# One core, windowed attention with sink tokens and a highway layer: ScalarE copy ahead of the second exponential, another start order, and crossbar transposes for eight blocks

## The chip, the cores and the metric

The kernel runs on one core of one Trainium2 chip. The metric is the device time of one execution in microseconds (us); less is better. A kernel is run several times, and each run has a span (first to last instruction, some 1.7 us less than the device time) and the mean clock that TensorE was granted, as a share of full speed. A stretch for which a trace holds no clock record counts as full in that mean and in the PEclk columns below. Runs over 1.5% above the fastest of the same kernel are set aside as slow. Engine names: PE is TensorE (matmuls and transposes by matmul), ACT is ScalarE, DVE is VectorE, POOL is GpSimd, SP is SyncE. PEld is PE's weight load, which overlaps PE. A "q" after the name (SPq, POOLq) is the engine's sequencer, which issues transfers.

## The reference

Attention with 4 sink positions and a window of 128, for 4 batches, 8 heads, 768 positions, head size 64; then a highway layer over 3072 tokens of 512 features.

```python
scores = q @ k.T / sqrt(64);  keep = is_sink | in_window
a = exp(scores - max) ; a = a / (sum(a) + 1e-9) ; x = a @ v          # x: 3072 x 512
H = maximum(x @ w_h, 0) ; T = 1 / (1 + exp(-(x @ w_t + b_t)))
out = T * H + (1 - T) * x
```

## The kernel before

The tokens are worked off in 24 blocks of 128, six to a batch. A block needs its own keys and those of the block before; the first of a batch has no block before, so its scores are half as large. Block n goes through these pieces:

| piece | engine | what it does | PSUM pool |
|---|---|---|---|
| T | PE, ACT copy `act_T` | transposes of q and k, copied to SBUF as `qk` | m |
| S, two halves | PE, ACT exponential `act_S`, DVE mask | scores, `e = exp(...)` | s |
| sk | PE, ACT short exponential | scores against the sinks, of two blocks at once | m |
| A | PE, then DVE `rec`, `x` | `e @ v`, division by the sum, giving `xh` | av |
| X | PE, ACT copy `act_X` | transpose of x, giving `xT` | m |
| Mt | PE, ACT tanh `act_u` | gate matmuls (`tps`) | m |
| Mh | PE, DVE `d`, `e`, `o` | candidate matmuls (`hps`), combination, store | m |

The engines take their instructions in the order in which the program lists them (weight loads aside), and the pool m has two buffers of one PSUM bank each that T, X, Mt, Mh and sk take in turn.

```python
s_ps  = ...tile_pool(name="ps_s",  bufs=2, space=PSUM)
av_ps = ...tile_pool(name="ps_av", bufs=1, space=PSUM)
m_ps  = ...tile_pool(name="ps_m",  bufs=2, space=PSUM)
...
for i in range(-2, NB + 2):                # a step; ms, os_: blocks whose Mt/Mh or d/e/o are due
    ...
    if has_sink(i): act_sink(i)
    if on(i + 1):
        pe_S(i + 1, 0); act_S(i + 1, 0); pe_S(i + 1, 1)
    if on(i - 1) and i - 1 not in XBAR:
        pe_X(i - 1); act_X(i - 1)
    for o in os_: dve_d(o)
    if on(i): dve_mask(i, 1)
    if on(i + 1): act_S(i + 1, 1)          # ACT: second exponential ...
    if on(i + 2): pe_T(i + 2)
    for o in os_: dve_e(o)
    if on(i): pe_A(i)
    if on(i + 2): act_T(i + 2)             # ... and only then the q,k copy
    if on(i + 1): dve_mask(i + 1, 0)
    if on(i): dve_rec(i)
    for o in os_: dve_o(o)
    if on(i):
        dve_x(i)
        if i in XBAR: sp_X(i)              # XBAR is empty here
    for m in ms:
        pe_Mt(m); act_u(m); pe_Mh(m)
    if has_sink(i + 1): pe_sink(i + 1)
    ...                                    # loads of block i + 10, POOL queue
```

(The `pe_` calls are shown several to a line; the start-up constants and the issue of the loads are cut.)

The softmax here doesn't subtract the row's maximum and nothing guards it: scores larger than these inputs give would overflow.

## Time and profile before

| what | before |
|---|---|
| time, median | 146.31 us |
| span of the profiled run | 145.0 us |
| six blocks in mid-run | 30.0 us |
| PE / ACT / DVE busy in these 30.0 us | 26.9 / 24.0 / 22.6 us |

The chain of waits of the kernel before, cut to one step in mid-run. Columns: start in us, length in us, what.

```profile
53.12 1.11 ACT e L251
54.23 0.47 ACT xT L315
54.71 1.02 ACT e L251
55.73 0.91 ACT qk L203
56.68 1.02 PE hps L336 x4
```

Four ACT instructions stand in a row, then PE's Mh (`hps`), and after it the next scores (in this step those against the sinks come first) start the next row. The list of waits of the kernel before shows the same tie from both ends. Columns: who waited for whom, us in total, times, longest us.

```profile
DVE dd L342 <- PE hps L336: 26.2, 24, 1.5
ACT e L251 <- PE sps L243: 12.7, 16, 0.9
PE hps L336 <- ACT qk L203: 9.4, 17, 0.7
```

Mh does not use the q,k copy's data. It waits for it because T and Mh take the same buffer of pool m in turn, and the copy is what frees it. While PE waits there, nothing releases ACT's next exponential, so ACT waits later.

Busy time by stretches of the kernel before. The columns are given in the first line.

```profile
core 0: us, PE busy (x) PEld busy (x) DVE busy (x) ACT busy (x) POOL busy (x), PEclk, DMA share, GB/s
43.40:73.40 30.00, 26.85 (x328) 17.65 (x328) 22.56 (x42) 23.96 (x32) 21.08 (x28) 1.00 1.87 170
73.40:103.40 30.00, 26.85 (x327) 17.66 (x326) 22.57 (x42) 23.96 (x32) 12.53 (x17) 1.00 0.98 106
```

The two stretches are six blocks each, with the same busy times. No engine is full (PE, the fullest, is busy for 26.85 of 30.00 us). The start is another matter; this is the timeline of the kernel before around the transposes of block 2.

```profile
11.04 1.04 PE L243 MATMUL sps<-qk 64*128 64x128 f16 x16 [1.10 <-ACT qk L203]
18.77 0.61 PE L196 MATMUL tp<-ident,qsd 128*128 128x128 f16 x4 [6.70 <-DMA qsd<-in_q_dram]
19.60 0.61 PE L198 MATMUL tp<-ident,ksd 128*128 128x128 f16 x4 [0.22 <-DMA ksd<-in_k_dram]
```

PE stands idle for 6.70 us until the q and k of block 2 have landed, although blocks 0 and 1 still have work that needs none of it.

### The profile page before, as it was taken

Reading aid. Unit: us, or ns where it says so; the run is one execution under the profiler, and the core shown is the slowest. Engines: PE = TensorE matmul, PEld = TensorE weight load, DVE = VectorE, ACT = ScalarE, POOL = GpSimd, SP = SyncE. Lnnn points to the kernel's source line nnn. Section 1 sums busy time; section 2 is a strip of 40 time slices with the busy share of each in tenths; the row PEclk is TensorE's granted clock in tenths of the full one; section 3 lists DMA queues with packets and bytes.
Section 4 is the critical chain, followed back from the end, with each engine's and each line's share of the span. In section 5 each row is a group of like instructions: output and inputs, shape, how many; then the busy total and the mean of one; then the engine's idle time right before and its main releaser. Section 6 shows DMA issues by size and latency. Waiting matters only on the chain.

```text
span 145.0 us, 3266 instructions
## 1 busy us (share of the span) xinstructions
PE 115.4 (80%) x1312; PEld 74.8 (52%) x1312; DVE 96.9 (67%) x214; ACT 98.0 (68%) x129; POOL 73.6 (51%) x98
## 2 busy tenths in 40 slices
PE   6632069989889988988899789889897988998840
PEld 2122058557646654765666358458464664664410
DVE  7441016578659856966868687678677866968770
ACT  3176029497787877977976797798769778976310
POOL 6999599999969999735099770000300000000000
PEclk9975555899999999999999999999999999999996
DMA  1999999999999999999929999210221021021111
GB/s 10 113 112 168 165 155 158 153 156 197 163 190 195 191 183 150 195 194 152 74 74 147 150 197 161 73 73 3 75 77 72 1 77 72 0 77 72 72 72 72
DMA packets 79728, 17.00 MB, mean 117 GB/s; under 512 B 75617, under 2 KB 76641, under 8 KB 79714
## 3 DMA queue, kind: packets, MB, share of 16 engines
q0 software_dynamic: 76256, 10.51, 107.8%
q1 hardware_dynamic: 3458, 6.30, 12.1%
q8 instruction: 10, 0.16, 0.4%
q14 instruction: 4, 0.03, 0.1%
HBM read 21.01 MB, written 6.29 MB: 188 GB/s over the span
## 4 chain that ended last, share of the span: by engine, by line
ACT 41%; PE 35%; POOL 7%; DMA 5%; issue 5%; DVE 4%; POOLq 0%; DVEq 0%
ACT e L251 25%; PE hps L336 16%; ACT qk L203 11%; DMA ksd<-in_k_dram 5%; PE tps L323 4%; ACT xT L315 4%; PE av L277 4%; PE sps L243 4%; DVE dd L342 3%; PE sk L221 3%; POOL qsd L85 2%; PE tps L321 1%; POOL ksd L86 1%; POOL v L93 1%; PE tp L198 1%
## 5 line engine op out<-in xcount | busy, mean ns | idle before, releaser
L251 ACT ACTIVATE e<-sps,ebias 128x1024 f16<-128x1024 f32 (+1 forms) x48 | 49.8, 1041 | 12.7 <-PE sps L243 12.7
L342 DVE SCALAR_TENSOR_TENSOR dd<-hps,xh 128x512 f16<-128x512 f32 x24 | 16.6, 692 | 26.2 <-PE hps L336 26.2
L262 DVE TENSOR_TENSOR e<-e,mask 128x1024 f16<-128x1024 f16 (+1 forms) x48 | 30.7, 640 | 4.4 <-ACT e L251 4.0
L203 ACT COPY qk<-tp 128x1024 f16<-128x1024 f16 x24 | 24.3, 1015 | 11.7 <-PE tp L198 11.7
L336 PE MATMUL hps<-wh_sb,xT 128*128 128x512 f16 x96 | 24.6, 378 | 9.4 <-ACT qk L203 9.4
L85 POOL DMA_DIRECT2D qsd<-in_q_dram x24 | 22.4, 932 | 7.6 <-PE tp L198 5.0
L323 PE MATMUL tps<-wt_sb,xT 128*128 128x512 f16 x96 | 25.0, 383 | 0.0
L277 PE MATMUL av<-v,e 128*128 128x112 f16 x352 | 24.4, 218 | 0.7 <-DVE e L262 0.7
L86 POOL DMA_DIRECT2D ksd<-in_k_dram x24 | 22.2, 925 | 1.1 <-PE av L283 1.0
L93 POOL DMA_DIRECT2D v<-in_v_dram x24 | 22.5, 937 | 0.0
L277 PEld LDWEIGHTS <-e 128*128 128x128 f16 x352 | 21.3, 101 | 1.1 <-DVE e L262 0.9
L336 PEld LDWEIGHTS <-xT 128*128 128x128 f16 x96 | 9.3, 97 | 23.5 <-issue 14.1
L329 ACT ACTIVATE u<-tps 128x512 f16<-128x512 f32 x24 | 14.7, 613 | 6.9 <-PE tps L323 6.8
L243 PE MATMUL sps<-qk 64*128 64x128 f16 x352 | 14.8, 225 | 2.6 <-ACT qk L203 2.6
L348 DVE SCALAR_TENSOR_TENSOR ee<-u,dd 128x512 f16<-128x512 f16 x24 | 16.5, 686 | 0.2
L296 DVE TENSOR_TENSOR xh<-av,rec 128x512 f16<-128x512 f32 x24 | 16.4, 685 | 0.1
L196 PE MATMUL tp<-ident,qsd 128*128 128x128 f16 x96 | 9.9, 230 | 7.2 <-DMA qsd<-in_q_dram 6.9
L354 DVE SCALAR_TENSOR_TENSOR otok<-xh,ee 128x512 f32<-128x512 f16 x24 | 15.6, 648 | 0.1
L243 PEld LDWEIGHTS <-qk 64*128 64x128 f16 x352 | 10.7, 98 | 9.4 <-issue 7.3
L323 PEld LDWEIGHTS <-xT 128*128 128x128 f16 x96 | 9.5, 99 | 11.0 <-issue 1.8
L315 ACT COPY xT<-xtp 128x512 f16<-128x512 f16 x24 | 13.7, 572 | 1.0 <-PE xtp L310 1.0
L212 POOL COPY ks<-qk 64x16 f16<-64x16 f16 x8 | 1.6, 201 | 21.1 <-ACT qk L203 20.9
(49 smaller groups left out, 103.3 us busy)
## 6 DMA issues: line engine op xcount, KB each, us to landing
out_dram<-otok SPq DMA_DIRECT2D x24, 256.0 KB, 2.2
qsd<-in_q_dram POOLq DMA_DIRECT2D x24, 128.0 KB, 5.7
ksd<-in_k_dram POOLq DMA_DIRECT2D x24, 128.0 KB, 5.7
v<-in_v_dram POOLq DMA_DIRECT2D x24, 128.0 KB, 6.1
wt_sb<-in_moe_w_t_dram POOLq DMA_DIRECT2D x1, 512.0 KB, 6.7
wh_sb<-in_moe_w_h_dram POOLq DMA_DIRECT2D x1, 512.0 KB, 8.8
vd<-in_v_dram POOLq DMA_DIRECT2D x4, 4.0 KB, 4.2
bt<-in_moe_b_t_dram SPq DMA_DIRECT2D x1, 2.0 KB
```

The lines of the kernel that those rows point to most:

```text
L85: nc.gpsimd.dma_start(out=qsd, in_=q[b, :, rows, :].transpose([1, 0, 2]))
L86: nc.gpsimd.dma_start(out=ksd, in_=k[b, :, rows, :].transpose([1, 0, 2]))
L93: nc.gpsimd.dma_start(out=vt[:, :, 0:D], in_=v[b, :, rows, :].transpose([1, 0, 2]))
L203: nc.scalar.copy(out=qk, in_=tp_of.pop(n))
L243: nc.tensor.matmul(sps[:, hh, o:o + P], lhsT=kk[rows, hp, :], rhs=qT[rows, hp, :], start=True, stop=True)
L251: nc.scalar.activation(out=e.rearrange("p a b c d -> p a (b c d)"), in_=sps[:, :, 0:2 * np_ * P], func=AF.Exp, bias=ebias, scale=SCALE)
L262: nc.vector.tensor_tensor(out=ev, in0=ev, in1=m.unsqueeze(1).to_broadcast([P, 4, np_ * P]), op=ALU.mult)
L277: nc.tensor.matmul(av[:, g, 2 * hl + hh, 0:_AVN], lhsT=e[:, hh, hl, pc, :], rhs=vt[:, 65 * h:65 * h + _AVN], start=first, stop=False, skip ...
L315: nc.scalar.copy(out=xT, in_=xtp_of.pop(n))
L323: nc.tensor.matmul(tps, lhsT=xT[:, kc, :], rhs=wt_sb[:, kc, :], start=False, stop=(kc == NOC - 1))
L336: nc.tensor.matmul(hps, lhsT=xT[:, kc, :], rhs=wh_sb[:, kc, :], start=(kc == 0), stop=(kc == NOC - 1))
L342: nc.vector.scalar_tensor_tensor(out=dd, in0=h_of.pop(n), scalar=0.0, in1=xh_of[n], op0=ALU.max, op1=ALU.subtract)
```

## The change

Three things, as the diff has them: from step 2 on, ACT takes the q,k copy ahead of the second exponential; in the start, blocks 0 and 1 are carried on before the transposes of block 2; and blocks 14 to 21 have x transposed by a DMA through the crossbar (`sp_X`, present but unused before) instead of PE and an ACT copy. Such a block's Mt and Mh come one step later (lag 2).

```diff
--- before.py
+++ after.py
@@ -73,7 +73,7 @@
     NV = AHEAD + 4
     NS4 = H * NSINK
     KW = NHP * P + 32
-    XBAR = ()
+    XBAR = range(14, 22)
     v_ring = [const.tile([P, VW], FP16, tag=f"v{i}", name=f"v{i}") for i in range(NV)]
     qk_sd = {}
 
@@ -375,7 +375,7 @@
                 more_constants()
             if has_sink(i):
                 act_sink(i)
-            if on(i + 1):
+            if i >= 2 and on(i + 1):
                 pe_S(i + 1, 0)
                 act_S(i + 1, 0)
                 pe_S(i + 1, 1)
@@ -383,20 +383,20 @@
                 pe_X(i - 1)
                 act_X(i - 1)
             for o in os_:
-                dve_d(o)
+                if o not in dd_of:
+                    dve_d(o)
             if on(i):
                 dve_mask(i, 1)
-            if on(i + 1):
+            if i >= 2 and on(i + 2):
+                pe_T(i + 2)
+                act_T(i + 2)
+            if i >= 2 and on(i + 1):
                 act_S(i + 1, 1)
-            if on(i + 2):
-                pe_T(i + 2)
             for o in os_:
                 dve_e(o)
             if on(i):
                 pe_A(i)
-            if on(i + 2):
-                act_T(i + 2)
-            if on(i + 1):
+            if i >= 2 and on(i + 1):
                 dve_mask(i + 1, 0)
             if on(i):
                 dve_rec(i)
@@ -410,6 +410,20 @@
                 pe_Mt(m)
                 act_u(m)
                 pe_Mh(m)
+            if i == 1:
+                dve_d(0)
+                pe_T(2)
+                act_T(2)
+            if -1 <= i < 2:
+                for g in range(2):
+                    pe_S(i + 1, g)
+                    act_S(i + 1, g)
+                dve_mask(i + 1, 0)
+            if i < 2:
+                n = {-2: 0, -1: 1, 1: 3}.get(i)
+                if n is not None:
+                    pe_T(n)
+                    act_T(n)
             if has_sink(i + 1):
                 pe_sink(i + 1)
             if i == 0:
@@ -422,7 +436,7 @@
                     sink_v(b, nc.gpsimd)
                 if b + 1 < B:
                     load_sink_v(b + 1)
-            for n in (range(3, AHEAD + 1) if i == -2 else [i + 2 + AHEAD]):
+            for n in {-2: range(3, AHEAD + 1), 0: [], 1: [10, 11]}.get(i, [i + 2 + AHEAD]):
                 if n < NB:
                     if n > 3:
                         load_qk(n)
```

## The prediction

> **What bounds the kernel.** The chain of waits repeats one pattern per block in mid-run: PE scores (0.35 us to the first half), ScalarE first exponential 1.11, xT copy 0.47, second exponential 1.02, q,k copy 0.91, PE Mh (the hps matmuls) 1.02, next scores: 4.95 us, about 5.4 with sink scores. Its tie is the two rotating PSUM buffers of the m pool: Mh takes the buffer that the q,k copy frees, so PE idles (waits: hps <- q,k copy, 17 times, 9.4 us), then ScalarE idles until the next scores (exp <- sps, 16 times, 12.7 us). By stretches, six blocks take 30.0 us three times over (43.4 to 133.4), ScalarE busy 24.0, VectorE 22.6; no engine is full. Outside: 43.4 us of start, 11.6 of end. In the start the timeline has PE idle from 12.1 to 18.8: the transposes of block 2, landed at 18.8/19.6, stand in PE's in-order stream ahead of the remaining work of blocks 0 and 1.
>
> **What the change does.**
> 1. q,k copy before the second exponential: Mh waits one exponential (1.02) less; the wait of hps should vanish. New limits per block, from start-to-start times in the timeline: PE about 4.2 (scores .55, x transposes .24, q,k transposes .44, A .80 to 1.02, Mt 1.07, Mh .86, sink scores about .5 in two of six), ScalarE about 4.1, VectorE 3.8 plus its wait for Mh. I estimate 4.3 without sink, 5.0 with (sink scores need the buffer that tanh frees, and tanh now comes after the second exponential): mean 4.45 instead of 5.0. Over the 12 blocks before the crossbar ones, 6.5 us.
> 2. Blocks 0 and 1 first: A, Mt, Mh of block 0 and A of block 1 move into the idle stretch. First exponential of block 3 near 26 instead of 28.5: 2.5 us. Loads are issued every 2.6 us per block, faster than any pace here.
> 3. Crossbar for 8 blocks: PE loses .24, ScalarE .47 per block, and the m pool turns over three buffers per block instead of four. Pace about 4.0 (4.5 with sink), bound by PE and VectorE: 3 to 4 us beyond item 1. Added: 8 transfers of 128 KB. The Trainium skill, "Advanced Engine Details and Errata", X-Bar Transpose, says they are as fast as regular DMAs; output stores here land in 2.2 us (256 KB), so I expect 2 to 3.5 us; the lag of two gives about 6 us of room, when the loads are mostly done (DMA share about 0.1 after 103 us). The trace before has no such transfer. Cost: the lag leaves one block more in the tail, 1.5 to 2 us more than the present 16.4 from the last scores (block 23) to the end.
>
> **Sum.** Block 3 at 25.5, twelve blocks at 4.45 to 79, block 14's step 4.4, the empty step 3.8, six at about 4.15 to 112, tail 18: span about 130, time 131.5 us. Range 128 to 135.5. Faster by over 2%: 0.96; within: 0.03; slower: 0.01.
>
> **What would show it.** Step 1: hps <- q,k copy near zero; six blocks in 26 to 27.5 us between 40 and 80. Step 2: PE's idle stretch partly filled, block 3's first exponential near 26. Step 3: no PE wait on crossbar transfers, landing under 4 us, pace near 4.1 us there. The idle ahead of VectorE's dd shrinks from 1.1 us per block to a few tenths.
>
> **What would make it wrong.** Crossbar transfers slower than their 6 us of room, or holding up loads or stores: Mt waits for DMA, 135 or more. VectorE's chain (x, dd only after Mh, then the mask) becoming the loop: step 1 gives half. If sink steps fall to 4.6, 128.

## The result, and the profile after

The changed kernel takes 132.95 us in the median (132.01 to 133.51, 4 runs) against 146.31. The ratio is 0.9078, with a 95% interval of 0.9021 to 0.9135. A ratio here is the mean time of one kernel's fast runs over that of the other's fast runs of the same rounds, so it is not quite the ratio of the medians quoted. On another chip, the same kernel gave 0.9115. The result is correct in all runs.

The waits of the changed kernel, the counterparts of the lines above:

```profile
DVE dd L342 <- PE hps L336: 13.4, 21, 2.0
ACT e L251 <- PE sps L243: 6.1, 13, 0.7
```

There is no line "PE hps <- ACT qk" any more, and the other two waits are halved. The chain of waits of the changed kernel, one step in mid-run, and the next, which has sink scores (short pieces are cut):

```profile
53.51 0.55 PE sps L243 x16
54.07 0.33 PE xtp L310 x4
54.40 0.22 PE tp L196 x4
54.62 0.22 PE tp L198 x4
54.84 0.40 PE av L277 x8
55.35 0.40 PE av L277 x8
55.87 0.22 PE tps L321
56.08 0.86 PE tps L323 x4
56.94 0.86 PE hps L336 x4
57.81 0.35 PE sps L243 x8
58.18 1.07 ACT e L251
59.66 1.02 ACT qk L203
60.68 1.02 ACT e L251
61.70 0.50 ACT u L329
62.23 0.61 PE sk L221 x8
```

The step from 53.51 to 57.81 is now PE from end to end. In the next one the ACT row is back: the sink scores wait for the buffer that tanh (`u`) frees, and tanh now stands behind the second exponential, as the prediction said. So the limit has moved to PE's own work in part only: ACT has 57% of the chain in 43.4 to 73.4 us of the kernel before and 34% in 40.2 to 67.2 us of the changed one. The stretches of the changed kernel, two of six blocks ahead of the crossbar (they overlap) and six steps with it:

```profile
40.20:67.20 27.00, 26.27 (x330) 17.61 (x326) 22.44 (x43) 24.03 (x32) 25.50 (x31) 1.00 2.16 186
53.50:80.60 27.10, 26.38 (x329) 17.68 (x330) 22.55 (x43) 24.05 (x32) 23.68 (x29) 1.00 2.09 181
88.40:112.90 24.50, 24.46 (x296) 15.94 (x297) 21.33 (x41) 20.88 (x26) 1.42 (x3) 1.00 0.33 94
```

Six blocks cost 27.0 to 27.1 us instead of 30.0, with the same ACT and DVE work, and 24.5 with the crossbar. Around the transposes of block 2 (timeline of the changed kernel):

```profile
17.74 1.03 PE L336 MATMUL hps<-wh_sb,xT 128*128 128x512 f16 x4
18.64 0.40 PE L196 MATMUL tp<-ident,qsd 128*128 128x128 f16 x4
19.48 0.40 PE L198 MATMUL tp<-ident,ksd 128*128 128x128 f16 x4 [0.44 <-DMA ksd<-in_k_dram]
```

PE has already done Mh of block 0 and waits only 0.44 us. The transfers of the changed kernel (columns: what, queue, kind and count, median us from issue to landing):

```profile
out_dram<-otok SPq DMA_DIRECT2D x24, 256.0 KB, 3.9
xT<-xh SPq DMA_TRANSPOSE x8, 2.5
```

The crossbar transfers land in 2.5 us in the median (block 14's, issued while the last load was still landing, took 4.2), and no engine waits for one. The stores' median rose from 2.2 to 3.9 us. That looks like a cost of the crossbar and is none: a version without it (p12 below) has 4.3. Issue by issue, a store takes about 5.2 us from issue to landing while loads run and 2.0 us when they have ended, in before, p12 and the changed kernel alike. The two groups are almost equal in size, so a store or two more in the first is enough for the median to jump from one group to the other.

### The profile page after: what moved, and what is told of

The parts are those of the page before. It is cut to its first block, busy times and chain, and to the rows that moved or that the text cites. A ratio compares the mean times of both kernels' runs of the same rounds, so it can differ in the third digit from the quotient of the medians.

```text
span 131.2 us, 3224 instructions
## 1 busy us (share of the span) xinstructions
PE 113.0 (86%) x1280; PEld 73.3 (56%) x1280; DVE 96.7 (74%) x214; ACT 94.6 (72%) x121; POOL 74.5 (57%) x98
## 4 chain that ended last, share of the span: by engine, by line
PE 50%; ACT 23%; POOL 8%; DMA 6%; DVE 5%; issue 5%; POOLq 0%; DVEq 0%
ACT e L251 13%; PE hps L336 11%; PE tps L323 11%; PE av L277 8%; PE sps L243 7%; ACT qk L203 7%; DMA ksd<-in_k_dram 6%; PE sk L221 3%; PE tps L321 3%; PE tp L196 3%; ACT u L329 2%; PE tp L198 2%; PE av L283 2%; DVE dd L342 2%; POOL qsd L85 2%
## 5 line engine op out<-in xcount | busy, mean ns | idle before, releaser
L203 ACT COPY qk<-tp 128x1024 f16<-128x1024 f16 x24 | 24.2, 1010 | 6.8 <-PE tp L198 6.7
L277 PE MATMUL av<-v,e 128*128 128x112 f16 x352 | 25.0, 220 | 1.9 <-DVE e L262 1.9
L342 DVE SCALAR_TENSOR_TENSOR dd<-hps,xh 128x512 f16<-128x512 f32 x24 | 16.6, 691 | 13.5 <-PE hps L336 13.4
L198 PE MATMUL tp<-ident,ksd 128*128 128x128 f16 x96 | 9.8, 227 | 1.8 <-DMA ksd<-in_k_dram 1.7
L321 PE MATMUL tps<-bt,ones_row 128*128 128x512 f16 x24 | 9.4, 390 | 1.0 <-DVE dd L342 0.6
```

The source lines that it names most:

```text
L203: nc.scalar.copy(out=qk, in_=tp_of.pop(n))
L277: nc.tensor.matmul(av[:, g, 2 * hl + hh, 0:_AVN], lhsT=e[:, hh, hl, pc, :], rhs=vt[:, 65 * h:65 * h + _AVN], start=first, stop=False, skip ...
L342: nc.vector.scalar_tensor_tensor(out=dd, in0=h_of.pop(n), scalar=0.0, in1=xh_of[n], op0=ALU.max, op1=ALU.subtract)
```

## The experiments

### The three parts, alone and in pairs

Six kernels make the full table of the three parts. The edits are small:

```diff
 p1_order: the kernel before, with
-            if on(i + 1): act_S(i + 1, 1)
-            if on(i + 2): pe_T(i + 2)
+            if on(i + 2):
+                pe_T(i + 2)
+                if i >= 2: act_T(i + 2)
+            if on(i + 1): act_S(i + 1, 1)
 ... (the later act_T only for i < 2)
 p3_xbar:  the kernel before, with      XBAR = range(14, 22)
 p12:      the changed kernel, with     XBAR = ()
 p13:      p1_order, with               XBAR = range(14, 22)
 p23:      the changed kernel, with act_S(i + 1, 1) ahead of pe_T, and act_T after pe_A again
 p2_start: p23, with                    XBAR = ()
```

> Only the ScalarE order (q,k copy ahead of the second exponential from step 2 on); start and transposes as before. Theory A (Mh waits for the PSUM buffer that the q,k copy frees, so the order alone breaks the tie in every step): the wait of hps for the q,k copy is under 1 us in all, six blocks take 27.0 to 27.2 us in all three stretches, and about 20 steps gain 0.5 each: 136 to 137.5 us. Rival B (the tie is ScalarE's work per block, and order alone only shifts the wait to the exponentials; the gain of the change comes from fewer ScalarE copies with the crossbar and from the start): 143 us or more.

> Only the start (blocks 0 and 1 ahead of the transposes of block 2); old ScalarE order, no crossbar. Theory A: a constant saving of 2.5 to 3.5 us before step 2 and 30.0 us per six blocks afterwards as before: 143 to 144 us. Rival B (the start is bound by the landing of loads, and the work moved up only waits later): under 1 us, 145.5 or more.

> Only the crossbar transposes for blocks 14 to 21, old order and start. Theory A: the xT copy (0.47) leaves the chain of the old order in eight steps, 3.8 us, and the longer tail gives 1.5 to 2 us back: 144 to 145 us. If the crossbar alone were what removes the tie (rival B): 141 or less.

> The change without the crossbar (new order and new start). Theory A: saves 2 to 3.5 us less than the whole change in the crossbar's steps but has the shorter tail (1.8 us): 133.5 to 135 us, so that the crossbar is worth only 1 to 2 us net. Rival B: 140 or more. The store's landing, 2.2 us before and 3.9 after, goes back to about 2.2 if the crossbar is its cause; if it stays near 3.9, it comes from the loads or the faster pace.

> The change without its new start (new order and crossbar). If the parts add up (theory A), 2.5 to 3 us above the whole change: 135.5 to 136. If the new start were worth nothing or the later steps absorbed it (rival B): 133 to 134.

> The change with the old ScalarE order (new start and crossbar). Theory A: most of the gain is lost: 141 to 142.5 us, and the wait of hps for the q,k copy is back with some 15 to 20 times 0.5 us. Rival B (the crossbar breaks the tie): 136 or less.

| kernel | order | start | crossbar | median us | ratio to before (95%) |
|---|---|---|---|---|---|
| before | | | | 146.01 (job of p1, p2, p3, p12) and 146.13 (job of p13, p23) | 1 |
| p1_order | x | | | 136.31 | 0.9307 (0.9256 to 0.9358) |
| p2_start | | x | | 144.38 | 0.9875 (0.9833 to 0.9918) |
| p3_xbar | | | x | 144.00 | 0.9869 (0.9798 to 0.9940) |
| p12 | x | x | | 135.87 | 0.9284 (0.9239 to 0.9329) |
| p13 | x | | x | 133.88 | 0.9144 (0.9104 to 0.9185) |
| p23 | | x | x | 143.32 | 0.9760 (0.9697 to 0.9822) |
| changed | x | x | x | 132.95 | 0.9078 (0.9021 to 0.9135) |

The changed kernel's row is from the job of the result above. The expectations named four times that did not come: p12 and p23 were 0.8 to 0.9 us slower than the ranges of theory A, p2_start 0.4, and p13 was 1.6 us faster than its range, inside that of its rival (the later steps absorb the gain of the start; see "Start").

**Order.** Alone it gives 9.7 us of the 13.4. Added last (p23 to changed) it gives 10.4 by the medians and some 10.0 by the ratios (an estimate across jobs). Its wait is gone in p1_order too: the list has no line for `hps` waiting for the q,k copy. In p23 and p3_xbar, which keep the old order, it is there. The waits of p23:

```profile
ACT e L251 <- PE sps L243: 12.3, 16, 0.9
PE hps L336 <- ACT qk L203: 7.6, 15, 0.9
```

Rival B, that the crossbar or the lighter ACT load breaks the tie, expected 143 or more for p1_order and 136 or less for p23; it has fallen. The crossbar takes the 0.47 us xT copy out of the row but leaves Mh tied to the last copy in it. No run changed the number of buffers in pool m; that the tie is the pool, and not some other link to the copy, rests on the program and on sink_late below, where T waits for an exponential whose result it does not read.

**Crossbar.** By the medians it gives 2.0 us alone, 1.1 with the start, 2.4 with the order and 2.9 with order and start. The traces say where. I took the start of each block's first exponential from the timelines and subtracted:

```
us                         exp of block 3   block 3 to 15   15 to 23   23 to the end
before                         28.54           60.05          40.38        16.03
p1_order                       27.83           54.26          36.47        16.04
p3_xbar                        27.65           60.05          36.03        17.83
p13                            27.63           54.26          32.31        17.81
p12                            26.34           55.25          36.46        16.05
changed                        25.65           55.40          32.30        17.83
```

Between blocks 15 and 23 the crossbar saves 4.2 us with the new order (36.5 to 32.3) and 4.4 with the old, and at the end it gives 1.8 back. The sum is 2.4 us with the new order and 2.6 with the old, so these two terms add; the wider scatter of the medians comes, in the profiled runs, from the start.

**Start.** It gives 1.6 us alone, but only 0.7 on top of the crossbar, 0.4 on top of the order and 0.9 on top of order and crossbar, where I had put 2.5. The table shows both halves of the miss. With the old start, block 3's first exponential comes at 28.54 in the profiled run of before, but at 27.6 to 27.8 in p1_order, p3_xbar and p13, whose start is the same program; I had read my baseline from a slow start. In that run the half clock lasts until 26.1 us and the step from block 2 to 3 takes 6.58 us; in the three others the matmuls change to full rate at 23.5 to 24.2 us and the step takes 5.44 to 5.48. And after the new start, blocks 3 to 15 take 1.0 to 1.1 us more (55.25 and 55.40 against 54.26). Nearly all of that is in the step from block 3 to block 4: 5.40 in changed and 5.24 in p12, against 4.26 in p13. The stretches between these two exponentials, first p13, then changed:

```profile
27.63:31.89 4.26, 4.26 (x61) 2.91 (x55) 3.47 (x7) 3.98 (x7) 4.26 (x6) 1.00 2.42 156
```

```profile
25.65:31.05 5.40, 5.40 (x63) 3.93 (x59) 2.39 (x5) 4.21 (x5) 5.40 (x8) 0.79 2.43 155
```

The PEclk column is 1.00 in the first and 0.79 in the second, and PE is busy from end to end in both, so a low clock costs time directly. That it is the clock and not the new order is shown by p2_start and p23, which run the same instructions there (the crossbar starts at block 14). First p2_start, then p23:

```profile
26.43:31.35 4.92, 4.42 (x61) 2.90 (x55) 2.39 (x5) 3.98 (x6) 4.92 (x7) 1.00 2.43 155
```

```profile
26.42:33.04 6.62, 6.62 (x63) 4.55 (x59) 2.39 (x5) 4.10 (x5) 6.62 (x9) 0.64 2.42 154
```

The same step takes 4.92 us at clock 1.00 and 6.62 at 0.64. The clock records cover this step in all runs, and the sizes fit. In the changed kernel half clock is recorded from 24.50 to 27.91 us, in its second profile (after_again, below) from 25.10 to 31.92. The step overlaps these by 2.26 and 4.88 us. Half of that is 1.13 and 2.44 us, and against the 4.32 us that start_t3 (below) takes at full clock the step lost 1.08 and 2.35.

The Trainium skill, "TensorE: Matmul & The Clock Gate", Part 1, says that the clock is gated to half or full by how busy PE has been recently. The traces agree as far as they go: all recorded shares are 0.5 or 1.0, and apart from the end of the span the recorded low stretches lie in the first 32 us, where PE is idle most (in the changed kernel it is busy for 1.59 us of the 4.50 ahead of the stretch at 24.50). The page adds that the time of the warm-up varies from run to run, because the window in which activity is counted runs freely. Here the stretch between 24 and 32 us is missing in p2_start and start_t3, 3.4 us long in the changed kernel and 6.8 us in p23 and after_again; whether the free-running window is the whole reason no run of mine settles.

The mean clock of a run does not show this. Among the traces, means near 0.99 come from those whose records begin late. In p1_order (mean 0.996) this line of the timeline lies where PEclk says 1.00 for want of a record:

```profile
21.70 1.04 PE L243 MATMUL sps<-qk 64*128 64x128 f16 x16 [0.35 <-ACT qk L203]
```

The same 16 matmuls take 1.04 us in the kernel before at a recorded 0.50, and 0.62 in mid-run, so PE was at half clock there too. And the kernel before took 145.92 us at a mean of 0.928 and 145.94 at 0.997 in one job. Of the changed kernel's first four runs, the one at 0.996 has a span of 130.3 us and the three at 0.935 to 0.946 have 131.2 to 131.8; it may have had no second low stretch, but its mean alone does not show that.

### Sink scores placed later: a theory of mine that fell

In the changed kernel a step with sink scores takes 5.07 us and one without 4.1 to 4.5. I took 0.3 us of that for PE's wait for the PSUM buffer that tanh frees, and moved the sink matmuls.

```diff
-            if has_sink(i): act_sink(i)
             if i >= 2 and on(i + 1):
                 pe_S(i + 1, 0); act_S(i + 1, 0); pe_S(i + 1, 1)
+            if has_sink(i):
+                pe_sink(i); act_sink(i)
 ...
-            if has_sink(i + 1): pe_sink(i + 1)
```

> The changed kernel, with the sink scores of a block moved from the end of the step before to after the scores of the next block. In the trace after, a step with sink scores takes 5.03 us from scores to scores and one without 4.29, of which 0.44 are the sink matmuls themselves; the other 0.3 are PE's wait for the buffer that tanh frees. If that is so, 0.25 to 0.3 us at each of 8 sink steps: 1.5 to 2.5 us below the change, 130.5 to 131.5. If the extra time is something else (the short exponential on ScalarE ahead of the long one): no gain.

It got slower: 137.03 us, ratio 0.9348 (0.9292 to 0.9404), some 3.5 to 4 us above the changed kernel. Timeline of sink_late in a step with sink scores:

```profile
55.06 1.11 ACT L251 ACTIVATE e<-sps,ebias 128x1024 f16<-128x1024 f32 x1
56.07 0.45 ACT L226 ACTIVATE es<-sk,ebias 32x256 f16<-32x256 f32 x1
56.57 0.38 PE L196 MATMUL tp<-ident,qsd 128*128 128x128 f16 x4 [0.56 <-ACT es L226]
```

The wait for tanh has become a longer one: T now takes the buffer of the sink scores, and their exponential stands behind the long one (1.11 us) in ACT's order, so PE waits 0.56 us instead of 0.30. The waits of T for that exponential sum to 2.8 us. Taken by first exponentials, the loss is 1.5 us between blocks 4 and 16 (55.7 against 54.2), 1.0 in the tail (18.87 against 17.82) and 1.35 in the step from block 3 to 4 (6.75 against 5.40), where the clock is not separated from the edit. Where a piece sits in the rotation of the two buffers matters as much as its own wait.

### The crossbar for blocks 4 to 21

```diff
-    XBAR = range(14, 22)
+    XBAR = range(4, 22)
```

> The changed kernel with crossbar transposes for blocks 4 to 21 instead of 14 to 21, so that ten of them fall in the time in which the loads keep the DMA engines full. If loads and transposes do not disturb each other, the ten steps gain about 0.4 us each: 129 us. If the transposes queue behind the loads (my prediction's reserve: slower than 6 us of room), PE waits for them, landing is over 5 us for the early ones, and the time is 133 or more.

The median is 136.67 us; two of four runs are slow, and the two fast ones are 134.33 and 135.46 (ratio 0.9209). So it is slower than the changed kernel although ten more blocks are relieved of 0.24 us of PE and 0.47 us of ACT work. Waits of xbar_4_22:

```profile
PEld L323 <- DMA xT<-xh: 7.3, 7, 2.4
PE tps L323 <- DMA xT<-xh: 4.8, 5, 2.1
```

Transfers of xbar_4_22:

```profile
out_dram<-otok SPq DMA_DIRECT2D x24, 256.0 KB, 5.3
qsd<-in_q_dram POOLq DMA_DIRECT2D x24, 128.0 KB, 7.3
xT<-xh SPq DMA_TRANSPOSE x18, 7.3
```

With loads about, a crossbar transfer lands in 6.9 to 7.9 us instead of 2.5 (twelve of the eighteen, so the median is 7.3), past the room of about 6 us that a lag of two gives, and PE waits. The loads suffer as well: q lands in 7.3 us in the median, against 6.2 in the changed kernel, and a store issued amid them in some 6.3 against 5.2. The Trainium skill, "Advanced Engine Details and Errata", X-Bar Transpose (TRN2), says that such transposes are as fast as regular DMAs. Times from issue to landing are near each other in both regimes: 2.5 us against the stores' 2.0 without loads, and 7.3 against some 6.3 amid them. But a store here moves 256 KB and a transpose 128 KB, so per byte no run shows the transpose to be as fast. Transposes are slowed by the other transfers as stores are. A range that starts at 14 avoids this: the transfer of block 14 is issued at 84.56 us in the changed kernel, when the last load is landing.

### What the longer tail is

```diff
-    XBAR = range(14, 22)
+    XBAR = range(14, 20)
```

> The changed kernel with the crossbar for blocks 14 to 19 instead of 14 to 21, so that the step with two highway blocks comes two steps earlier and out of the tail. If the longer tail (17.8 us from block 23's first exponential to the end, 16.0 without crossbar) is the step with two highway blocks, the tail is 16.0 again, the step with two costs 1.8 to 2 more earlier, and two steps lose 0.4: 133.5 to 134, no better. If the longer tail has another cause, it stays 17.8: 134 or more.

134.70 us, ratio 0.9202 (0.9155 to 0.9248), against 133.6 for the fast runs of the changed kernel on the same chip, so not faster. The tail from block 23's first exponential is 16.20 us instead of 17.82, and the step before it is 7.01 instead of 4.59. So the tail's extra time is the step in which two blocks' Mt and Mh come together, after the lag goes back from two to one; moved forward it costs more than at the end.

### Two starts

The yardstick on the same chip is the changed kernel again.

> The changed kernel itself once more, on the same chip as the three others, as their yardstick: 132 to 133.5 us, about 1 us apart by the granted clock between 15 and 30 us (no theory hangs on it).

It gave 133.84 us in the median of six runs, 133.6 in that of the four fast ones; two are slow. Its profiled run is one of the slow ones, with clock 0.63 in the step from block 3 to 4 (6.67 us), so nothing is read from its start but the step from block 2 to 3 and that low clock.

The first candidate applies the change's own idea to its start:

```diff
 (step 1)
-                for g in range(2): pe_S(2, g); act_S(2, g)
-                dve_mask(2, 0)
-                pe_T(3); act_T(3)
+                pe_S(2, 0); act_S(2, 0); pe_S(2, 1)
+                dve_mask(2, 0)
+                pe_T(3); act_T(3)
+                act_S(2, 1)
```

> The changed kernel with the change's own order also in its start: block 3's transposes and q,k copy ahead of the second exponential of block 2. In the trace after, PE waits 1.8 us for that copy ahead of the sink scores. If the start is bound by the chain landing of block 2 -> copy -> scores -> two exponentials -> copy -> sink scores, block 3's first exponential comes 0.8 us earlier (24.8) and the time falls by 0.5 to 0.9. If the landing of block 3 or 4 binds instead: no gain.

131.54 us (130.50 to 132.28, 6 runs), ratio 0.8982 (0.8936 to 0.9029). It beats both kernels. From block 2's first exponential to block 3's it takes 3.28 us, against 4.24 in both profiled runs of the changed kernel: 0.96, near the 0.8 expected; the kernel's time fell by more than the 0.5 to 0.9 expected. The timeline of start_t3 there:

```profile
22.04 1.11 ACT L251 ACTIVATE e<-sps,ebias 128x1024 f16<-128x1024 f32 x1 [0.49 <-PE sps L243]
23.05 1.01 ACT L203 COPY qk<-tp 128x1024 f16<-128x1024 f16 x1
23.95 1.12 ACT L251 ACTIVATE e<-sps,ebias 128x1024 f16<-128x1024 f32 x1
24.11 0.38 PE L221 MATMUL sk<-qk,ks 128*128 128x128 f16 x4 [0.88 <-ACT qk L203]
```

PE's wait for the copy is 0.88 instead of 1.82 us. The medians of the fast runs on this chip lie 2.1 us apart, more than this step explains. The rest of the profiled difference is the step from block 3 to 4, which was at full clock here (4.32 us against 5.40 in the changed kernel's fast profile). Whether the new order in the start brings that full clock or only met it in this run is open: one profile is not enough, and the mean clocks cannot tell (the two runs of start_t3 at 0.996 and 0.998 have spans of 130.1 and 130.6 us, longer than the 128.8 to 129.9 of the four at 0.950 to 0.956).

The second candidate changes the order of loads in the changed kernel (it does not have the reorder of start_t3):

```diff
+        load_qk(2); load_v(2)
         load_w(moe_w_t, wt_sb); load_w(moe_w_h, wh_sb)
 ...
-        load_qk(2); load_v(2)
         load_qk(3)
 (step 1: T and S of block 2 ahead of Mt and Mh of block 0)
```

> The changed kernel with block 2's loads issued ahead of the two weight loads, and its transposes and scores ahead of Mt and Mh of block 0. If the start is bound by the order of landings, block 2 lands near 15 instead of 19.5, block 3's first exponential comes near 23.5 instead of 25.6, and the time falls by 1 to 2.5 us. If the late weights (about 18 and 20.5 instead of 15 and 17.7) push Mt and Mh into the stretch in which PE is the limit, the gain is under 0.5 or there is none.

132.36 us, ratio 0.9030 (0.8987 to 0.9073): no better than start_t3, and some 1.3 us below the fast runs of the changed kernel, with intervals that overlap a little. Block 2's first exponential does come early, at 19.28 us, but block 3's comes at 25.67, no sooner than in the changed kernel. Its step of 6.39 us holds Mt and Mh of block 0, which now run from 19.60 to 23.3 and stand ahead of T of block 3 (23.11) in PE's order. They take 3.7 us there, at a recorded half clock (until 22.8 us), where mid-run takes 1.9. The early landing was spent on the same serial work a little later. The gain that it has over the changed kernel is, in the profiles, the step from block 3 to 4 at full clock (4.26 us instead of 5.40), which I had not aimed at. So the time came out inside the expected gain of 1 to 2.5 us, but not by the earlier landing: that is luck.

## Why the prediction was right

The time forecast was 131.5 us with a range of 128 to 135.5; 132.95 was measured, and the forecast of a clear gain held. Point by point:

- **Step 1, order: right.** The wait is gone; six blocks take 27.0 to 27.1 us, inside the 26 to 27.5 named. The step estimates were 4.3 us without sink and 5.0 with; the trace has 4.1 to 4.5 and 5.07, and the named reason for the longer one, sink scores that wait for tanh, is in the chain. The term "twelve blocks, 6.5 us" measured 5.8 (60.05 to 54.26 in p1_order). Taken alone over all its steps, the order is worth 9.7 us.
- **Step 2, start: right mechanism, size too large.** "2.5 us" measured 1.6 alone and 0.4 to 0.9 with the order. First, the baseline of 28.5 came from a profiled run with a longer half clock in the start; other runs of the same start have 27.6 to 27.8. Second, in the step from block 3 to 4 PE is the limit and fell back to half clock in most profiles of the new start (5.40 us instead of 4.26). That block 3 came at 25.65, as forecast, looks better than it is, since the gain was counted from the slow baseline.
- **Step 3, crossbar: right, both terms.** "3 to 4 us" measured 4.2 between blocks 15 and 23, "1.5 to 2 us" of longer tail measured 1.8, and 2 to 2.9 us net. Landing was put at 2 to 3.5 us, with none over 4, and measured 2.5 in the median and 4.2 for block 14. The named risk, transfers slower than 6 us when loads are about, was made to happen with blocks 4 to 21: PE waits for them, and the fast runs take 134.3 and 135.5 us where 135 or more was named.
- **The sum.** Block 3 at 25.5 (25.65 for its exponential), tail 18 (17.82 from the exponential), span about 130 (131.2). What is missing is mainly the low-clock step and a pace of 4.52 instead of 4.45.
- **The idle ahead of `dd`** went from 26.2 to 13.4 us in all, about 1.1 to 0.56 per block: "a few tenths" was too hopeful. It is idle time of an engine that was not the limit: in 40.2 to 67.2 us DVE has 5% of the chain, ACT 34% and PE nearly all the rest.

## What to carry to other kernels

When PSUM buffers rotate, an instruction can wait for a copy whose data it never reads; look for a wait between two pieces that share only a pool, and put the copy that frees the buffer ahead of work that nothing waits for soon. This reorder was worth 9.7 of 13.4 us and left every engine's work the same. Moving work to the DMA engines paid here only where they had room: the same transfer landed in 2.5 us after the loads and 7.3 us amid them. Read a baseline in the start of a kernel from several runs, since one profiled run can hold a low clock that the next does not. And check a clock column against the durations of equal matmuls, since a trace without clock records reads as full speed.

## What the Trainium skill lacked or had wrong

- "Advanced Engine Details and Errata", X-Bar Transpose (TRN2): gives speed in proportion to other DMAs, but no landing time for a small transpose from SBUF to SBUF, nor that it queues with loads. Here 128 KB took 2.5 us from issue to landing on an otherwise quiet queue, of which SP's issue alone is 1.2 us (0.34 for a plain store of 256 KB), and some 7.3 us amid loads.
- "TensorE: Matmul & The Clock Gate", Part 1: says that the warm-up varies from run to run and, for modelling, costs under 1% of a typical span. The first holds here. The second does not hold in every run: a later return to half clock alone cost 1.1 us of 131.2 in one profile of the changed kernel and 2.4 of 133.9 (1.8%) in the other (estimates, against 4.32 us for the same step at full clock in start_t3). The page also lacks the warning that this is as large as what a reworked start gains: one step of identical instructions took 4.92 or 6.62 us, and one profiled run of the kernel before put block 3 at 28.54 where others have 27.6 to 27.8.
- No page that I read says that a median of landing times can jump with the share of transfers that meet other traffic: stores landed 2.0 us or about 5.2 us after issue, and the median went from 2.2 to 3.9 us with neither value changed.
